# Routing products and key-value sums moved ahead in the head pairs of an attention and mixture-of-experts kernel

## The chip, the cores and the metric

The kernel runs on one core of a Trainium2 chip. A core has five engines that work through their own instruction lists in parallel: TensorE (PE; its weight loads are listed apart as PEld), VectorE (DVE), ScalarE (ACT), GpSimd (POOL) and SyncE (SP, which here only issues DMAs). The metric is the device time of one execution in microseconds (us); lower is better.

## The reference

The inputs are q, k and v of 8 batches x 8 heads x 576 positions x 64, and a 128 x 64 matrix omega. Attention is the linear kind with random features:

```python
def phi(x):
    proj = np.einsum('bhsd,md->bhsm', x, omega)
    sq = np.sum(x * x, axis=-1, keepdims=True) / 2.0
    h = proj - sq
    h = h - np.max(h, axis=-1, keepdims=True)
    return np.exp(h) / np.sqrt(m)
q_p, k_p = (phi(q_s), phi(k_s))
kv = np.einsum('bhsm,bhsd->bhmd', k_p, v)
z = np.sum(k_p, axis=2)
num = np.einsum('bhsm,bhmd->bhsd', q_p, kv)
den = np.einsum('bhsm,bhm->bhs', q_p, z)[..., None] + 1e-06
```

The 4608 rows of num / den go to a mixture of 8 experts: gate logits by a 512 x 8 matrix, the best expert of each row, and for that expert `np.maximum(xe @ w1[e], 0.0) @ w2[e]` with a hidden width of 1024, scaled by the gate's softmax weight.

## The kernel before

The program has two stages. The attention stage fills roughly the first 260 us of the profiled span, the expert stage the rest. All five engines have an order written out by hand: each engine runs its instructions in the order in which the Python code emits them, and waits at an instruction until what it needs is there.

**Units.** Attention works on 72 units, nine for each of the batches 0 to 7: one unit for the 64 last positions of all heads (h = -1), then one for each head's first 512 positions. A unit passes through these steps:

- `turns` (L148): TensorE transposes raw k and q of a later unit, and the q features of an earlier one, into the PSUM tile tt; `copies` (L183): ScalarE copies tt to SBUF.
- `unit_p` (L200): TensorE projects onto omega, into the tile pp (two buffers).
- `unit_m` (L213): VectorE takes the maxima mx (L217).
- `unit_e` (L220): ScalarE takes four exponentials for k (kp) or four for q (qp), all on line L229.
- `unit_ks` (L231): GpSimd sums the key features.

**Pairs.** `pair` (L382) handles two heads, u and w, and the work of earlier pairs beside them. Each batch has pairs k = 0 to 3, and before pair 0 a lone unit in `rest` (L368). Batch 0 has only its pairs 2 and 3 in this form, so there are 30 pairs. For pair p, `pair_kv` (L250) makes the key-value sums of pair p - 1 on TensorE in the PSUM bank "kv", and `pair_kvt` (L267) copies them out on ScalarE. `pair_fold` (L274) multiplies the copied sums of pair p - 2 by the gate matrix and the identity in the bank "nu", and copies that to SBUF as kva on ScalarE. `numbers` runs `pair_nu` (L291), two sets of numerators on TensorE, one in the bank "nu" and one in the bank "kv", and `pair_x` (L307), the divisions on VectorE that empty these banks. Each bank exists once, so every one of these steps waits until the step before it in the same bank has been read.

**Routing steps.** When a batch's rows are done (at the end of pair 1 of the next batch), its routing is put in a queue of small steps (`group`, L542): s0 copies or reduces the logits and takes the maximum, s5 subtracts and has ScalarE take an exponential (ex, L603), s1 and s2 build the one-hot choice, s3 counts ranks with TensorE products (rr) and reads them on VectorE, s4 and s6 finish rank and gate weight and write the weight to DRAM, and one step per row block builds the tile RH (two VectorE instructions). An odd batch has 12 steps and its s0 has a TensorE product (rf), an even one has 11. Batch 3 adds eight steps that choose the first expert. Steps with a TensorE product are in the set `pe`; their product uses the bank "nu". `some` takes steps from the queue:

```python
def some(self, n, products=True):
    while n and self.queue and (products or self.queue[0] not in self.pe):
        self.queue.pop(0)()
        n -= 1
```

So `some(n, False)` stops at the next step with a product. The pair takes a product step, if one is at the head of the queue, and then up to three more.

**Between the stages.** `rest` of the experts (L868) issues 6 of the first expert's 32 layer-one products per its `fill`, then all routing steps that are left but the last batch's last six, then 4 products, then those six; after that 22 products follow (L849), and the slots of all rows are worked out.

Of the kernel before, what the change touches and what calls it, by code (L numbers as in the profile page):

```python
# [57 lines left out]
class Attention:  # L58
# [309 lines left out]
    def rest(self, i, b, pre):  # L368

        rt, u = self.routing, self.units[i]  # L370
        pre.ahead(i - len(self.units))
        self.unit_p(*u)
        self.unit_m(*u)
        self.turns(i + 3, i - 2)
        self.copies(i + 3, i - 2)
        self.numbers(b * NP - 3)
        self.unit_e(*u, 0)
        self.unit_e(*u, 1)
        self.unit_ks(*u)
        rt.some(1, False)  # L380

    def pair(self, i, p, pre):  # L382

        rt, (u, w) = self.routing, self.units[i:i + 2]
        for k in range(2):
            pre.ahead(i + k - len(self.units))
        self.unit_p(*u)
        self.unit_m(*u)
        self.turns(i + 3, i - 2, pre)
        self.copies(i + 3, i - 2, pre)  # L390
        self.pair_fold(p - 2)
        self.unit_e(*u, 0)
        self.pair_kv(p - 1)
        self.unit_e(*u, 1)
        self.unit_ks(*u)
        if rt.queue and rt.queue[0] in rt.pe: rt.some(1)
        rt.some(3, False)
        self.unit_p(*w)
        self.unit_m(*w)
        self.pair_kvt(p - 1)  # L400
        self.turns(i + 4, i - 1, pre)
        self.copies(i + 4, i - 1, pre)
        self.unit_e(*w, 0)
        self.unit_e(*w, 1)
        self.unit_ks(*w)
        if p % NP < NP - 1 or p == B * NP - 1: self.numbers(p - 2)
# [718 lines left out]
```

## Time and profile before

| | |
|---|---|
| median of 3 runs | 722.06 us (721.88 to 723.95) |
| the profiled execution | 723.1 us, span from first to last instruction 721.4 us |
| mean granted TensorE clock | 0.992 |
| busy over the span | PE 678.3, PEld 610.7, DVE 342.1, ACT 352.7, POOL 255.5 us |

A row of a timeline gives the start from the beginning of the span, the duration, the engine, the line of the kernel, the operation, the tiles written and read, shapes, and how many instructions are merged. Brackets at the end say how long the engine sat idle before and what released it. On ScalarE and VectorE an instruction may start while the last one drains, so distances between starts say how fast the engine works, and durations overlap. The name of a releaser is inferred: a wait put down to `DVE de L312` ended with what stood on VectorE just then.

### The profile page before, as it was taken

Reading aid. Unit: us, or ns where it says so; the run is one execution under the profiler, and the core shown is the slowest. Engines: PE = TensorE matmul, PEld = TensorE weight load, DVE = VectorE, ACT = ScalarE, POOL = GpSimd, SP = SyncE. Lnnn points to the kernel's source line nnn. Section 1 sums busy time; section 2 is a strip of 40 time slices with the busy share of each in tenths; the row PEclk is TensorE's granted clock in tenths of the full one; section 3 lists DMA queues with packets and bytes.
Section 4 is the critical chain, followed back from the end, with each engine's and each line's share of the span. In section 5 each row is a group of like instructions: output and inputs, shape, how many; then the busy total and the mean of one; then the engine's idle time right before and its main releaser. Section 6 shows DMA issues by size and latency. Waiting matters only on the chain. (4 is left out here: it accounts for less than half of the span.)

```text
span 721.4 us, 19765 instructions
## 1 busy us (share of the span) xinstructions
PE 678.3 (94%) x7569; PEld 610.7 (85%) x7569; DVE 342.1 (47%) x790; ACT 352.7 (49%) x961; POOL 255.5 (35%) x459
## 2 busy tenths in 40 slices
PE   6899989889898989999999998999999999999995
PEld 5788879788887877888999888988989989988994
DVE  3367887788788778722221145112245245122220
ACT  6899989989989925311221144111234144111210
POOL 7456556545556632221222212211203303212221
PEclk9999999999999999999999999999999999999998
DMA  7846346627644521551112126101135125201000
GB/s 208 241 149 193 118 116 188 188 70 199 200 128 158 183 69 47 179 175 32 48 50 63 35 88 225 60 33 61 47 132 185 60 90 183 91 33 33 18 32 22
DMA packets 69506, 79.89 MB, mean 111 GB/s; under 512 B 28398, under 2 KB 52974, under 8 KB 69360
## 3 DMA queue, kind: packets, MB, share of 16 engines
q1 hardware_dynamic: 61136, 58.81, 26.5%
q0 software_dynamic: 7680, 19.04, 8.0%
q8 instruction: 87, 1.43, 0.8%
q14 instruction: 59, 0.48, 0.2%
q10 hardware_dynamic: 544, 0.13, 0.1%
HBM read 64.79 MB, written 19.55 MB: 117 GB/s over the span
## 5 line engine op out<-in xcount | busy, mean ns | idle before, releaser
L939 PE MATMUL p<-xh,w1p 128*128 128x256 f32 (+2 forms) x1104 | 156.2, 284 | 0.9 <-ACT xh L52 0.9
L939 PEld LDWEIGHTS p<-xh,w1p 128*128 128x128 f32 x1104 | 143.3, 188 | 3.0 <-ACT xh L52 1.3
L981 POOL DMA_INDIRECT out_dram<-ys,idx x36 | 36.5, 1014 | 299.9 <-DVE ys L980 207.5
L958 DVE SCALAR_TENSOR_TENSOR hl<-p,hh 128x512 fp32r<-128x512 f32 (+1 forms) x76 | 50.1, 662 | 130.1 <-ACT hh L957 128.1
L957 ACT ACTIVATE hh<-p 128x512 fp32r<-128x512 f32 (+1 forms) x76 | 43.6, 575 | 137.1 <-PE p L939 132.8
L217 DVE TENSOR_REDUCE mx<-pp 128x8 f32<-128x1024 f32 x64 | 78.0, 1219 | 32.1 <-PE pp L210 29.8
L229 ACT ACTIVATE kp<-pp,mx 128x128 f32<-128x128 f32 x256 | 86.2, 576 | 13.0 <-DVE de L312 8.6
L939 PE MATMUL p<-xl,w1p 128*128 128x256 f32 (+2 forms) x552 | 88.9, 283 | 0.0
L229 ACT ACTIVATE qp<-pp,mx 128x128 f32<-128x128 f32 x256 | 87.6, 607 | 0.0
L210 PE MATMUL pp<-om_t,tq 64*128 64x128 f32 x1024 | 74.3, 284 | 7.2 <-ACT qp L229 6.4
L245 POOL TENSOR_TENSOR k<-kp 128x256 f32<-128x256 f32 x64 | 46.5, 727 | 92.8 <-ACT kp L229 87.0
L939 PEld LDWEIGHTS p<-xl,w1p 128*128 128x128 f32 x552 | 75.7, 188 | 0.0
L210 PEld LDWEIGHTS pp<-om_t,tq 64*128 64x128 f32 x1024 | 62.1, 187 | 14.1 <-ACT qp L229 7.9
L188 ACT COPY tq<-tt 128x1024 f32<-128x1024 f32 x59 | 72.9, 1235 | 2.2 <-PE tt L146 2.2
L966 PE MATMUL p_t<-w2p,hh 128*128 128x512 f32 x152 | 61.6, 405 | 2.3 <-DVEq L986 1.9
L968 PE MATMUL p_t<-w2p,hl 128*128 128x512 f32 x152 | 60.3, 397 | 0.0
L967 PE MATMUL p_t<-w2p,hh 128*128 128x512 f32 x152 | 60.1, 395 | 0.0
L979 ACT ACTIVATE ys<-p_snu,gt 128x256 f32<-128x256 f32 x18 | 8.5, 474 | 91.9 <-PE p L939 55.5
L968 PE MATMUL p_snu<-w2p,hl 128*128 128x512 f32 x136 | 53.3, 392 | 0.0
L966 PE MATMUL p_snu<-w2p,hh 128*128 128x512 f32 x136 | 53.2, 391 | 0.0
L967 PE MATMUL p_snu<-w2p,hh 128*128 128x512 f32 x136 | 53.2, 391 | 0.0
L980 DVE TENSOR_SCALAR ys<-p_snu,gt 128x256 f32<-128x256 f32 x18 | 8.7, 484 | 85.8 <-ACT ys L979 85.8
(368 smaller groups left out, 1226.2 us busy)
## 6 DMA issues: line engine op xcount, KB each, us to landing
w1s<-in_moe_w_dram SPq DMA_DIRECT2D x5, 2048.0 KB, 8.7
w2s<-in_moe_w_dram SPq DMA_DIRECT2D x5, 2048.0 KB, 11.3
v<-in_v_dram SPq DMA_DIRECT2D x32, 256.0 KB, 4.9
token_rows<-xc SPq DMA_DIRECT2D x8, 1024.0 KB, 4.8
k<-in_k_dram SPq DMA_DIRECT2D x31, 256.0 KB, 4.9
q<-in_q_dram SPq DMA_DIRECT2D x31, 256.0 KB, 5.1
kr<-in_k_dram SPq DMA_DIRECT2D x16, 64.0 KB, 3.2
vz<-in_v_dram SPq DMA_DIRECT2D x16, 64.0 KB, 4.2
```

The lines of the kernel that those rows point to most:

```text
L188: self.nc.scalar.copy(self.pack(i, j), tt)
L210: nc.tensor.matmul(pp[:, a, n, i, :], th[r, k].rearrange("p a t -> p (a t)"), self.om[r, :], start=True, stop=True)
L217: nc.vector.tensor_reduce(out=mx[:, :, n], in_=s[("pp", h)][:, :, n], axis=AX.X, op=ALU.max, negate=True)
L229: nc.scalar.activation(x[:, j, :], pp[:, j % 2, n, j // 2, :], AF.Exp, bias=mx[:, j % 2, n, j // 2:j // 2 + 1])
L245: add = lambda o, x, y: nc.gpsimd.tensor_tensor(out=o, in0=x, in1=y, op=ALU.add)
L939: self.nc.tensor.matmul(o, w[:, i, c], x[:, i, :], start=k == 0, stop=k == len(ops) - 1)
L957: self.nc.scalar.activation(a, o, AF.Relu)
L958: self.nc.vector.scalar_tensor_tensor(out=b, in0=o, scalar=0.0, in1=a.bitcast(F32), op0=ALU.max, op1=ALU.subtract)
L966: nc.tensor.matmul(p, h, self.w2h[:, c, :], start=c == 0, stop=False)
L967: nc.tensor.matmul(p, h, self.w2l[:, c, :], start=False, stop=False)
L968: nc.tensor.matmul(p, l, self.w2h[:, c, :], start=False, stop=c == self.NF - 1)
L981: self.nc.gpsimd.indirect_dma_start(out=self.out[:, :], in_=y, in_offset=None, bounds_check=NT - 1, out_offset=bass.IndirectOffsetOnAxis(a ...
```

## The change

In `pair`, the routing steps move from behind the first unit's exponentials to a place ahead of the key-value sums, and a product step now counts among the three. `pair_kv` and its copy `pair_kvt` are emitted ahead of the fold; the copies of the sums and of the fold now stand on ScalarE between u's k exponentials and its q exponentials. In `rest` up to two steps without a product are taken, where one was.

```diff
--- before.py
+++ after.py
@@ -377,7 +377,7 @@
         self.unit_e(*u, 0)
         self.unit_e(*u, 1)
         self.unit_ks(*u)
-        rt.some(1, False)
+        rt.some(2, False)
 
     def pair(self, i, p, pre):
 
@@ -388,16 +388,17 @@
         self.unit_m(*u)
         self.turns(i + 3, i - 2, pre)
         self.copies(i + 3, i - 2, pre)
+        products = bool(rt.queue) and rt.queue[0] in rt.pe
+        rt.some(int(products))
+        rt.some(3 - products, False)
+        self.pair_kv(p - 1)
+        self.unit_e(*u, 0)
+        self.pair_kvt(p - 1)
         self.pair_fold(p - 2)
-        self.unit_e(*u, 0)
-        self.pair_kv(p - 1)
         self.unit_e(*u, 1)
         self.unit_ks(*u)
-        if rt.queue and rt.queue[0] in rt.pe: rt.some(1)
-        rt.some(3, False)
         self.unit_p(*w)
         self.unit_m(*w)
-        self.pair_kvt(p - 1)
         self.turns(i + 4, i - 1, pre)
         self.copies(i + 4, i - 1, pre)
         self.unit_e(*w, 0)
```

ScalarE, batch 4, pair 2 and the start of pair 3. tq is the copy of the transposed tile, ex the routing exponential, the other names as above. Before:

```order
L188 COPY tq_39_3271<-tt_39_3254 128x2x8x64
L288 COPY kva_3282<-fold_3273 128x146
L229 ACTIVATE kp_4_3284<-pp_4_3243,mx_4_3252 128x128 x4
L229 ACTIVATE qp_4_3300<-pp_4_3243,mx_4_3252 128x128 x4
L603 ACTIVATE ex_3318<-sh_3316 128x40
L271 COPY kvt_3340<-kv_3289 128x256
L188 COPY tq_40_3359<-tt_40_3342 128x2x8x64
L229 ACTIVATE kp_5_3361<-pp_5_3329,mx_5_3338 128x128 x4
L229 ACTIVATE qp_5_3366<-pp_5_3329,mx_5_3338 128x128 x4
L188 COPY tq_41_3433<-tt_41_3416 128x2x8x64
```

With the change, the same stretch and on into pair 3:

```order
L188 COPY tq_39_3269<-tt_39_3252 128x2x8x64
L229 ACTIVATE kp_4_3284<-pp_4_3241,mx_4_3250 128x128 x4
L271 COPY kvt_3289<-kv_3273 128x256
L288 COPY kva_3300<-fold_3291 128x146
L229 ACTIVATE qp_4_3302<-pp_4_3241,mx_4_3250 128x128 x4
L188 COPY tq_40_3340<-tt_40_3323 128x2x8x64
L229 ACTIVATE kp_5_3342<-pp_5_3312,mx_5_3321 128x128 x4
L229 ACTIVATE qp_5_3347<-pp_5_3312,mx_5_3321 128x128 x4
L188 COPY tq_41_3414<-tt_41_3397 128x2x8x64
L604 ACTIVATE ex_3424<-sh_3422 128x40
L229 ACTIVATE kp_6_3442<-pp_6_3386,mx_6_3395 128x128 x4
L271 COPY kvt_3447<-kv_3431 128x256
```

kvt and kva stand between kp and qp, and ex, which stood behind both sets of exponentials of pair 2, now stands in pair 3 ahead of kp_6.

TensorE, batch 4, pair 0, from the transposes of u to the projection of w (the products of s3 are rr, of which the first stands at the end here). Before:

```order
L146 MATMUL tt_35_2924<-ident,qp_7_2813 128x64 x8
L283 MATMUL fold_2943<-G,kvt_2787 64x72 x4
L286 MATMUL fold_2943<-ones,ks_2_2613 64x1 x4
L264 MATMUL kv_2959<-kp_6_2746,v_1690 64x128 x4
L264 MATMUL kv_2959<-kp_-1_2211,vz_158 64x128
L264 MATMUL kv_2959<-kp_-1_2211,vz_159 64x128
L264 MATMUL kv_2959<-kp_7_2808,v_1690 64x128 x4
L578 LDWEIGHTS rt_tri
L578 MATMUL rr_2980<-rt_OH,rt_tri 128x32
```

With the change, from the second-last product of s3, whose first follows the transposes `tt_35` at once:

```order
L582 LDWEIGHTS rt_ones
L582 MATMUL rr_2943<-rt_OH,rt_ones 128x16
L582 LDWEIGHTS rt_ones
L582 MATMUL rr_2943<-rt_OH,rt_ones 128x8
L264 MATMUL kv_2964<-kp_6_2750,v_1688 64x128 x4
L264 MATMUL kv_2964<-kp_-1_2181,vz_158 64x128
L264 MATMUL kv_2964<-kp_-1_2181,vz_159 64x128
L264 MATMUL kv_2964<-kp_7_2808,v_1688 64x128 x4
L283 MATMUL fold_2982<-G,kvt_2755 64x72 x4
L286 MATMUL fold_2982<-ones,ks_2_2617 64x1 x4
L210 MATMUL pp_1_3003<-om_t,tq_33_2806 128x128 x8
```

The products have moved ahead of sums and fold; the sums come behind them and the fold last.

VectorE between the stages: what stands ahead of the last batch's first step, the copy of rf into rt_L. Before, the end of the row-block steps:

```order
L628 TENSOR_SCALAR rt_RH_90<-rt_iob_93,rt_RM_89,rt_ihi_122 128x128
L628 TENSOR_SCALAR rt_RH_90<-rt_iob_93,rt_RM_89,rt_ilo_123 128x128
L628 TENSOR_SCALAR rt_RH_90<-rt_iob_93,rt_RM_89,rt_ihi_122 128x128
L628 TENSOR_SCALAR rt_RH_90<-rt_iob_93,rt_RM_89,rt_ilo_123 128x128
L558 COPY rt_L_85<-rf_7_5849 128x8
L560 TENSOR_REDUCE l_mx_5853<-rt_L_85 128x5
L601 TENSOR_TENSOR l_sh_5859<-rt_L_85,l_mx_5853 128x40
```

With the change, the stretch behind the last reduction of attention:

```order
L629 TENSOR_SCALAR rt_RH_90<-rt_iob_93,rt_RM_89,rt_ihi_122 128x128
L629 TENSOR_SCALAR rt_RH_90<-rt_iob_93,rt_RM_89,rt_ilo_123 128x128
L561 TENSOR_REDUCE mx_6_5805<-rt_L_85 128x4
L602 TENSOR_TENSOR sh_6_5807<-rt_L_85,mx_6_5805 128x32
L565 TENSOR_TENSOR w_6_5811<-rt_L_85,mx_6_5805 128x32
L566 TENSOR_TENSOR w_6_5811<-w_6_5811,rt_rev_95 128x32
L568 TENSOR_REDUCE mw_6_5814<-w_6_5811 128x4
L571 TENSOR_TENSOR rt_OH_86<-w_6_5811,mw_6_5814 128x32
L573 TENSOR_REDUCE cs_6_5817<-rt_OH_86 128x8
L574 TENSOR_TENSOR rt_CU_87<-rt_CU_87,cs_6_5817 128x8
L586 TENSOR_TENSOR m_6_5826<-rr_6_5820,rt_OH_86 128x32
L588 TENSOR_REDUCE rk_6_5828<-m_6_5826 128x4
```

Ahead of `COPY rt_L<-rf_7` there are now 29 instructions behind attention's last reduction, where there were 8: the whole group of batch 6 has moved here, with its product and its exponential.

## Rows read from the trace of the kernel before

**Rows 1.** Stretch 60 to 100 us: length, then busy PE, PEld, DVE, ACT, POOL; clock.

```profile
60.00:100.00 40.00, 36.19 (x756) 33.02 (x753) 31.70 (x80) 36.03 (x114) 21.23 (x42) 1.00 0.46 131
```

**Rows 2.** Groups by line, 60 to 250 us: busy, mean ns, idle before and releasers.

```profile
L229 ACT ACTIVATE kp<-pp,mx 128x128 f32<-128x128 f32 x197 | 66.0, 564 | 12.9 <-DVE de L312 8.6 <-DVE mx L217 4.3
```

**Rows 3.** Timeline of ScalarE, batches 1 to 7; mostly batch 4.

```profile
41.98 1.32 ACT L188 COPY tq<-tt 128x1024 f32<-128x1024 f32 x1
...
138.77 1.14 ACT L229 ACTIVATE kp<-pp,mx 128x128 f32<-128x128 f32 x4 [1.38 <-DVE de L312]
...
140.78 1.06 ACT L188 COPY tq<-tt 128x1024 f32<-128x1024 f32 x1
...
143.85 0.51 ACT L271 COPY kvt<-kv 128x256 f32<-128x256 f32 x1
...
144.10 1.17 ACT L188 COPY tq<-tt 128x1024 f32<-128x1024 f32 x1
...
147.01 1.24 ACT L188 COPY tq<-tt 128x1024 f32<-128x1024 f32 x1
...
147.91 0.53 ACT L288 COPY kva<-fold 128x146 f32<-128x146 f32 x1
...
148.08 1.40 ACT L229 ACTIVATE kp<-pp,mx 128x128 f32<-128x128 f32 x4
...
150.38 0.26 ACT L603 ACTIVATE ex<-sh 128x40 f32<-128x40 f32 x1
...
153.10 1.14 ACT L229 ACTIVATE kp<-pp,mx 128x128 f32<-128x128 f32 x4 [1.30 <-DVE de L312]
...
229.27 1.14 ACT L188 COPY tq<-tt 128x1024 f32<-128x1024 f32 x1
```

**Rows 4.** Timeline of VectorE, batch 4.

```profile
131.36 1.23 DVE L217 TENSOR_REDUCE mx<-pp 128x8 f32<-128x1024 f32 x1
...
134.44 0.19 DVE L585 TENSOR_TENSOR m<-rr,rt_OH 128x32 f32<-128x32 f32 x1 [1.86 <-PE rr L581]
...
137.47 1.21 DVE L217 TENSOR_REDUCE mx<-pp 128x8 f32<-128x1024 f32 x1
...
145.60 0.46 DVE L314 TENSOR_TENSOR x<-nu,de 128x288 f32<-128x288 f32 x1
...
149.14 0.17 DVE L558 COPY rt_L<-rf 128x8 f32<-128x8 f32 x1 [1.17 <-PE rf L557]
...
151.79 1.22 DVE L217 TENSOR_REDUCE mx<-pp 128x8 f32<-128x1024 f32 x1
```

**Rows 5.** Timeline of TensorE, batch 4.

```profile
134.14 0.18 PE L578 MATMUL rr<-rt_OH,rt_tri 128*128 128x32 bf16 x1 [0.68 <-ACT kva L288]
...
144.42 0.73 PE L301 MATMUL nu<-kva,tq 128*64 128x73 f32 x16 [0.32 <-ACT kvt L271]
...
145.07 1.16 PE L210 MATMUL pp<-om_t,tq 64*128 64x128 f32 x16
...
146.31 0.42 PE L146 MATMUL tt<-ident,qp 64*128 64x64 f32 x8
...
146.66 0.47 PE L283 MATMUL fold<-G,kvt 128*64 128x72 f32 x8
...
147.17 0.64 PE L264 MATMUL kv<-kp,v 128*64 128x128 f32 x8
...
148.49 0.61 PE L557 MATMUL rf<-lr,rt_fold 128*128 128x8 f32 x4
...
149.03 1.16 PE L210 MATMUL pp<-om_t,tq 64*128 64x128 f32 x16
```

**Rows 6.** Timeline of VectorE between the stages.

```profile
266.12 0.17 DVE L558 COPY rt_L<-rf 128x8 f32<-128x8 f32 x1 [0.76 <-PE rf L557]
...
267.36 0.20 DVE L570 TENSOR_TENSOR rt_OH<-l_w,l_mw 128x40 bf16<-128x40 f32 x1
```

**Rows 7.** Timeline of TensorE between the stages.

```profile
268.10 9.74 PE L849 MATMUL p<-x,w1s 128*128 128x256 f32 x44
```

## The prediction

> **What bounds the kernel now.** I read the busy time by stretches first. In attention PE and ACT are equally busy, 36.2 and 36.0 of 40 us, and DVE is at 31.7 [rows 1]. So no engine is full, and the question is who waits for whom. The groups by line answer it for ScalarE: nearly all of its idle time stands ahead of one group, the k exponentials, 12.9 us in 190, and what it waits for is VectorE [rows 2].
>
> The timeline of ScalarE then shows what it does when it doesn't wait. From the copy at 140.78 to the copy at 147.01, one pair, it runs at 6.23 us; from 144.10 to 147.01, one unit without extras, at 2.91 [rows 3]. Six batches lie between the copies at 41.98 and 229.27, that is 187.3 us. At ScalarE's own pace they would take 6 x (4 x 6.23 + 2.91) = 167.0; six routing exponentials last 0.26 each, 1.6, partly over their neighbours, so I add 1.1: 168.1. 19.2 us are lost there, and that is all that a better order in the loop can give.
>
> Where it goes is seen in batch 4. Stall A: kp at 138.77 waits 1.38 us (and the copies ahead of it already started late), stall B: kp at 153.10 waits 1.30 [rows 3]; both for maxima that VectorE starts at 137.47 and 151.79 only [rows 4]. VectorE is late there because of routing: it waited 1.86 us for the products rr, worked through 11 small instructions, and only then took w's maximum; at B it waited 1.17 us for rf [rows 4]. And rr was late because its bank was freed by ScalarE's copy kva: PE stood 0.68 us idle for it [rows 5]. ScalarE waits for VectorE, which waits for TensorE, which waited for ScalarE.
>
> TensorE has its own small wait of this kind: the second numerators wait 0.32 us for kvt [rows 5], since kvt and they share a bank and kvt is copied only at 143.85, after the q exponentials [rows 3].
>
> **The change, part by part.**
>
> *Products first.* They now follow the transposes. At A these end where the maximum of u is being taken, from 131.36 for 1.23 us [rows 4], so rr is done before VectorE wants it, at 132.6 in place of 134.44. That takes 1.86 us off w's maximum; the step that leaves the pair takes two RH instructions more. A needs 1.38 + about 0.4, so it goes. At B the wait of 1.17 goes, and s2 leaves the pair; B goes too. A third place like A lies in pair 3 of the same batch. What is late next is ScalarE itself.
>
> *At most three steps, two in the lone unit.* Every pair has less routing between two maxima. Price: s2 now stands in the lone unit right ahead of pair 0, which also has s3. I take 0.3 us in each of three batches, 0.9 (bounds 0 and the 0.63 that s2's three instructions last at the spacing worked out below, so 0 to 1.9).
>
> *Sums before the fold, kvt ahead of q.* On TensorE the same work stands between the transposes of u and those of w, only in another order: fold 0.51 us (146.66 to 147.17), sums 1.32 (147.17 to 148.49), rf 0.54 [rows 5]. The second numerators' wait for kvt goes, so PE gets further ahead. ScalarE now reaches kvt 0.90 + 1.0 us after the start of the copy of u (147.01 to 147.91 for the copy, half of 138.77 to 140.78 for four exponentials), and kva 0.25 later (143.85 to 144.10) [rows 3]. The transposes end 0.28 ahead of that copy (146.31 + 0.42 against 147.01); sums, then fold end 1.83 us after them, so 1.55 after the copy's start, 0.6 ahead of ScalarE. With a product it is 0.54 more and the margin about nothing. I count no wait at the 19 pairs without a product, and 0.5 us in all at the 11 with one, for the 36 products of the first expert's choice above all (bounds 0 and 11 x 1.17, the wait that VectorE had for rf, if ScalarE inherits it: 12.9).
>
> *The routing exponential.* This is the cost that the description doesn't name: ex is emitted with its step, so it now stands on ScalarE ahead of u's k exponentials, six times in the loop. If VectorE is late, all of ScalarE stands. From rt_L at 149.14 to ex at 150.38 there are 1.24 us [rows 3, 4]. u's maximum at A's pair ended at 132.59 [rows 4], 0.8 before ScalarE wanted it, so 1.24 - 0.8 = 0.45 is lost when VectorE is on time, and 1.3 when it is as tight as at 148.08, just behind a maximum. I take 0.5 each, 3.0 in all (bounds 0 and 7.8).
>
> [...]
>
> *The end of attention.* With fewer steps per pair the queue runs late, and batch 6's whole group is left for the stretch between the stages. There VectorE has 21 instructions more ahead of rt_L. Six such steps took from 266.12 to 267.36, 0.21 each [rows 6]; 21 make 4.4, less the 0.76 that VectorE waited for rf anyway, 3.7. At the pace of the 11 instructions from 134.44 to 137.47, 0.28 [rows 4], it is 5.1. Nothing hides it: the next 22 expert products start at 268.10 [rows 7] behind the last batch's products, for which VectorE must first come to its one-hot choice; TensorE stands meanwhile. Gate-weight DMAs on SP's queue move by up to a batch with their steps; no load stands right behind one that needed it earlier, so I count them at nothing, and GpSimd's order is unchanged. The expert stage behind it is untouched and shifts as a whole.
>
> Sum: 19.2 - (0.9 + 0.5 + 3.0) = 14.8 gained in the loop, 3.7 lost behind it: 11.1. Against the profiled execution of 723.1 this gives 712.0, against the median of 722.06, 711.0. I predict **711.5**.
>
> **Rivals.**
>
> *Everything goes.* If TensorE, freed from kvt, gets far enough ahead that ex and the fold never hold ScalarE, 19.2 are gained: 723.1 - 15.5 = 707.6, or 706.6 by the median. For it: stretches like 138.77 to 150.38 already run without a wait. Against: TensorE's pair takes 3.42 (145.07 to 149.03 less rf) + 1.59 + 2 x 0.65 = 6.3 us, as much as ScalarE's, so it gains only in pair 3, which has no numerators.
>
> *The wait turns round (slower).* ScalarE's queue now holds two copies and ex ahead of exponentials, where before only VectorE stood. At the six ex 1.3 each, at the 11 pairs with a product 1.17 each: 20.7, more than the 19.2 that can go. With the 3.7 behind: 723.1 + 1.5 + 3.7 = 728, 727 by the median. It decides as soon as these 17 places lose more than 1.04 us each (17.7 in all, which leaves 1.5 against 3.7). Half of that, 0.5 to 1 each, ends near no change. For it: the margin of the fold with a product is nil. Against: in such a pair ex and fold wait for the same late VectorE, so their waits overlap, and a late ScalarE lets TensorE catch up.
>
> *The tail is worse.* If TensorE's products for batch 6 and the exchange with ScalarE double the 3.7, the time is 715, still faster.
>
> **How the numbers follow.** The forecast (with the worse tail) 0.66, its own range 707.5 to 719; everything goes 0.14, time 705.5 to 707.5; the wait turns round 0.20, of which 0.10 lands slower, 0.06 within the bound and 0.04 still faster. About 0.3% (2.2 us) is what a measurement tells from no change. A further 0.02 of the forecast lies between 719 and 720, within the bound. So faster 0.82, same 0.08, slower 0.10. The range from 705.5 to 720 leaves out the 0.10 that is slower, half of what lands within the bound, and some 0.03 below.
>
> **What would show it.** Right: the copies of batches 1 to 7 that stand at 41.98 and 229.27 come 12 to 17 us closer together; rr and rf no longer appear as VectorE's releasers for more than 0.3 us; kvt no longer appears ahead of the second numerators; ScalarE shows waits of 0.3 to 0.8 ahead of ex; rt_L between the stages comes 3.5 to 5 us later after attention's last reduction, with TensorE idle ahead of the last rr. Wrong: waits of over 1 us ahead of ex or kva, with the fold as releaser, at most pairs with a product; or k exponentials that still wait over 1 us for VectorE.

## The result and the profile after

The changed kernel takes 709.91 us (median of 4 runs, 708.92 to 714.09) against 723.0 of the kernel before in the same comparison (4 runs, 721.88 to 724.0). The ratio is 0.984, 95% interval 0.9815 to 0.9866: faster by 1.3 to 1.9%. The forecast was 711.5 (705.5 to 720). The profiled execution has 709.2 us and a span of 707.5; its mean granted clock is 0.996, against 0.992 before.

The stretch that answers to [rows 1] shows TensorE a little busier and ScalarE without a gap:

```profile
60.00:100.00 40.00, 36.98 (x795) 34.88 (x793) 31.11 (x82) 40.00 (x127) 24.22 (x48) 1.00 0.60 180
```

The groups of ScalarE by line, 60 to 235 us, answer to [rows 2]. The 12.9 us listed ahead of the k exponentials are 0.3, and neither of the two copies that moved ahead of the q exponentials has taken them over:

```profile
L229 ACT ACTIVATE kp<-pp,mx 128x128 f32<-128x128 f32 x194 | 72.1, 711 | 0.3 <-DVE mx L217 0.2
...
L271 ACT COPY kvt<-kv 128x256 f32<-128x256 f32 x24 | 16.5, 686 | 0.0
L288 ACT COPY kva<-fold 128x146 f32<-128x146 f32 x24 | 14.8, 617 | 0.0
```

ScalarE's timeline (start, duration), with the first and the last copy of the same rank as in [rows 3], and pairs 1 and 2 of batch 3 from 106.53 on:

```profile
40.10 1.42 ACT L188 COPY tq<-tt 128x1024 f32<-128x1024 f32 x1
...
106.53 0.80 ACT L288 COPY kva<-fold 128x146 f32<-128x146 f32 x1
106.69 1.68 ACT L229 ACTIVATE qp<-pp,mx 128x128 f32<-128x128 f32 x4
107.70 1.57 ACT L188 COPY tq<-tt 128x1024 f32<-128x1024 f32 x1
108.60 1.72 ACT L229 ACTIVATE kp<-pp,mx 128x128 f32<-128x128 f32 x4
...
110.61 1.65 ACT L188 COPY tq<-tt 128x1024 f32<-128x1024 f32 x1
112.01 1.29 ACT L229 ACTIVATE kp<-pp,mx 128x128 f32<-128x128 f32 x4
...
114.46 1.23 ACT L188 COPY tq<-tt 128x1024 f32<-128x1024 f32 x1
...
213.64 1.37 ACT L188 COPY tq<-tt 128x1024 f32<-128x1024 f32 x1
```

The two copies stand 173.54 us apart, where they stood 187.29: the loop gives 13.75. One wait shows without a bracket: kp starts 1.40 after its copy at 110.61, where 0.90 is the pace (107.70 to 108.60).

VectorE in the places that answer to [rows 4]: the end of that pair 1, and then stall A's place, pair 0 of batch 4:

```profile
108.28 0.17 DVE L312 TENSOR_SCALAR de<-nu 128x5 f32<-128x5 f32 x1 [0.32 <-PE nu L304]
...
110.05 0.62 DVE L526 TENSOR_REDUCE rt_L<-x 128x32 f32<-128x256 f32 x1
110.59 0.20 DVE L533 TENSOR_REDUCE lr<-x 128x8 f32<-128x32 f32 x1
110.70 1.21 DVE L217 TENSOR_REDUCE mx<-pp 128x8 f32<-128x1024 f32 x1
...
125.64 1.23 DVE L217 TENSOR_REDUCE mx<-pp 128x8 f32<-128x1024 f32 x1
126.78 0.18 DVE L586 TENSOR_TENSOR m<-rr,rt_OH 128x32 f32<-128x32 f32 x1
...
129.12 1.22 DVE L217 TENSOR_REDUCE mx<-pp 128x8 f32<-128x1024 f32 x1 [0.28 <-PE pp L210]
```

The read of rr at 126.78 follows u's maximum without a wait (before 1.86), and w's maximum starts 2.34 later, when its projection is there. TensorE, to [rows 5]: rr runs under u's maximum, sums and fold behind it; the second numerators wait for kvt only once more between 40 and 240 us (0.7), but the first ones now wait for kva.

```profile
107.38 0.73 PE L301 MATMUL nu<-kva,tq 128*64 128x73 f32 x16 [0.27 <-ACT kva L288]
...
125.95 0.19 PE L579 MATMUL rr<-rt_OH,rt_tri 128*128 128x32 bf16 x1
...
126.16 0.66 PE L264 MATMUL kv<-kp,v 128*64 128x128 f32 x8
...
127.31 0.42 PE L283 MATMUL fold<-G,kvt 128*64 128x72 f32 x8
```

Between the stages, to [rows 6, 7], attention's last logits reduction and the copy of rf on VectorE, then TensorE:

```profile
247.59 0.62 DVE L526 TENSOR_REDUCE rt_L<-x 128x32 f32<-128x256 f32 x1
...
254.11 0.46 DVE L559 COPY rt_L<-rf 128x8 f32<-128x8 f32 x1
```

```profile
251.38 1.97 PE L850 MATMUL p<-x,w1s 128*128 128x256 f32 x8
255.92 0.18 PE L579 MATMUL rr<-rt_OH,rt_tri 128*128 128x40 bf16 x1 [2.57 <-DVE rt_OH L571]
...
256.40 5.86 PE L850 MATMUL p<-x,w1s 128*128 128x256 f32 x26
```

From the reduction to the 22 products it is now 8.81 us; before it was 5.26, from this row to the products at 268.10 [rows 7]:

```profile
262.84 0.62 DVE L525 TENSOR_REDUCE rt_L<-x 128x32 f32<-128x256 f32 x1
```

So the 13.9 us between the two profiled executions come out as: loop 13.75 gained; between the stages 3.55 lost; from the last copy to attention's last reduction 0.38 lost (33.57 before, 33.95 now); ahead of the first copy 1.88 gained; from the 22 products to the end 2.2 gained (453.3 and 451.1). The last two aren't the change's: the rows at the end of this document with a clock of 0.57 and 0.72 belong to them. The order itself is worth some 10 us.

### The profile page after: what moved, and what is told of

It is laid out like the page before. It is cut to its first block, busy times and chain, and to the rows that moved or that the text cites. A ratio compares the mean times of both kernels' runs of the same rounds, so it can differ in the third digit from the quotient of the medians.

```text
span 707.5 us, 19748 instructions
## 1 busy us (share of the span) xinstructions
PE 668.1 (94%) x7569; PEld 607.3 (86%) x7569; DVE 339.7 (48%) x790; ACT 352.9 (50%) x961; POOL 255.8 (36%) x459
## 5 line engine op out<-in xcount | busy, mean ns | idle before, releaser
L229 ACT ACTIVATE qp<-pp,mx 128x128 f32<-128x128 f32 x256 | 96.3, 737 | 0.0
L229 ACT ACTIVATE kp<-pp,mx 128x128 f32<-128x128 f32 x256 | 93.8, 695 | 0.3 <-DVE mx L217 0.2
L188 ACT COPY tq<-tt 128x1024 f32<-128x1024 f32 x59 | 83.1, 1408 | 0.9 <-PE tt L146 0.9
```

The lines of the kernel that those rows point to most:

```text
L188: self.nc.scalar.copy(self.pack(i, j), tt)
L229: nc.scalar.activation(x[:, j, :], pp[:, j % 2, n, j // 2, :], AF.Exp, bias=mx[:, j % 2, n, j // 2:j // 2 + 1])
```

## The experiments

For each kernel the table has the median with its ratio to the kernel before and the 95% interval, then, from its profiled execution, the distance of the two copies ("loop"), and that from attention's last reduction to the 22 products ("tail").

| kernel | us | ratio | loop | tail |
|---|---|---|---|---|
| before | 721.6 to 723.6 | 1 | 187.29 | 5.26 |
| changed | 709.91 | 0.984 (0.9815 to 0.9866) | 173.54 | 8.81 |
| routing only | 715.93 | 0.9922 (0.9903 to 0.9941) | 177.84 | 8.83 |
| sums only | 732.26 | 1.0145 (1.0123 to 1.0166) | 200.48 | 5.26 |
| cap only | 723.53 | 1.0025 (1.0000 to 1.0049) | 180.29 | 8.82 |
| old counts | 709.82 | 0.9836 (0.9812 to 0.986) | 175.93 | 5.25 |
| reductions later | 709.92 | 0.9842 (0.982 to 0.9864) | 173.02 | 8.82 |
| ex behind | 713.45 | 0.9878 (0.9849 to 0.9907) | 173.14 | 10.09 |
| plan | 713.34 | 0.9876 (0.9857 to 0.9895) | 176.95 | 6.90 |
| plan, reductions early | 709.43 | 0.9828 (0.9805 to 0.985) | 176.01 | 5.25 |
| reductions later, ex behind | 711.35 | 0.985 (0.9825 to 0.9874) | 172.77 | 8.82 |
| plan, ex behind | 707.33 | 0.9795 (0.9772 to 0.9818) | 173.91 | 5.26 |

The runs of one kernel lie 1 to 7 us apart, so differences of 1 to 2 us are read from the two right columns.

### Taking the change apart

*Routing only* (against the kernel before):

```diff
-        rt.some(1, False)
+        rt.some(2, False)
...
+        products = bool(rt.queue) and rt.queue[0] in rt.pe
+        rt.some(int(products))
+        rt.some(3 - products, False)
         self.pair_fold(p - 2)
         self.unit_e(*u, 0)
         self.pair_kv(p - 1)
         self.unit_e(*u, 1)
         self.unit_ks(*u)
-        if rt.queue and rt.queue[0] in rt.pe: rt.some(1)
-        rt.some(3, False)
```

> Only the routing part of the change: the steps follow the transposes, at most three with a product counted, two in the lone unit; the fold, the key-value sums and their copies stay in their old order. Theory A (the parts need each other: the gain comes from VectorE no longer waiting for routing products; their bank must be free when they come, and the sums and kvt in front free TensorE): 716 us, range 712 to 720. The tail between the stages gets 3.6 us longer as in the changed kernel, the k exponentials keep about 0.3 to 0.5 us of wait per pair with a product, and the second numerators still wait for kvt. Theory B (the gain is the routing alone: the order of sums and fold is worth nothing): 709 to 711, as the changed kernel. Theory C (the gain is from kvt and the sums freeing TensorE, routing does nothing but lengthen the tail): 724 to 727.

Theory A, in the time, the tail and the wait for kvt. The waits that it saw ahead of the k exponentials aren't listed; instead the distance from u's copy to w's in pair 3 grows by up to 0.9 us. In the waits of TensorE, 40 to 240 us (engine and line, waited for; total, times, longest), a new one is on top:

```profile
PE fold L283 <- DVE m L586: 5.7, 6, 1.3
PE nu L301 <- ACT kvt L271: 2.8, 4, 0.8
```

rr stands in the bank "nu" ahead of the fold now, so the fold waits until VectorE has read rr, and sums and projection of w queue behind it. The second row is the old wait for kvt.

*Sums only* (against the changed kernel):

```diff
-        rt.some(2, False)
+        rt.some(1, False)
...
-        products = bool(rt.queue) and rt.queue[0] in rt.pe
-        rt.some(int(products))
-        rt.some(3 - products, False)
...
         self.unit_ks(*u)
+        if rt.queue and rt.queue[0] in rt.pe: rt.some(1)
+        rt.some(3, False)
         self.unit_p(*w)
```

> Only the other part: key-value sums and kvt ahead of the fold and of the q exponentials; the routing steps at their old place and in their old number. The fold's copy kva now comes about 1.25 us later than before, and the routing products wait for it in the same bank. Theory A: the loop gets slower, 725 to 732 us, with VectorE waiting over 2.5 us ahead of the first read of the routing products and the k exponentials of w waiting for that; the tail between the stages stays as short as before. Theory B (routing alone is the gain): 721 to 724, no change. Theory C (the sums are the gain): 706 to 710, since the tail isn't lengthened.

Theory A again, just above its range: the same instructions, 10 us slower than before. Waits of TensorE and VectorE, 40 to 240 us:

```profile
PE rr L578 <- ACT kva L288: 9.2, 6, 2.1
```

```profile
DVE m L585 <- PE rr L581: 15.3, 6, 3.2
```

Before, TensorE's rr waited 0.68 at the place shown [rows 5]; with kva behind kp and kvt it waits up to 2.1, and VectorE up to 3.2. So the two halves are not two gains. Moved alone, the routing products hold the fold; moved alone, the fold holds the routing products. Together the product is in front, the sums fill the time in which VectorE reads it, and the fold finds the bank free (127.31 above, without a wait).

A part of this loss is the clock. The first of these waits of rr, and the granted clock (third-last column) just behind it:

```profile
71.64 0.18 PE L578 MATMUL rr<-rt_OH,rt_tri 128*128 128x32 bf16 x1 [2.05 <-ACT kva L288]
```

```profile
73.20:76.60 3.40, 3.40 (x52) 3.13 (x50) 3.16 (x13) 2.17 (x7) 0.00 (x0) 0.50 0.18 28
```

Five such stretches lie in this loop, none in that of the kernel before. u's interval in pair 2, from its copy to w's, takes 6.04 us in the batch in which one of them falls there, and 5.38 and 5.39 in two without. At this 0.66 each, they would be some 3 of the 13.2 us that the loop grew, an estimate; the rest is the waits themselves.

*Cap only* (the kernel before with the change's numbers of steps):

```diff
-        rt.some(1, False)
+        rt.some(2, False)
...
-        if rt.queue and rt.queue[0] in rt.pe: rt.some(1)
-        rt.some(3, False)
+        products = bool(rt.queue) and rt.queue[0] in rt.pe
+        rt.some(int(products))
+        rt.some(3 - products, False)
```

> The old order of everything; only the number of routing steps is that of the changed kernel, three in a pair with the product among them, two in the lone unit. Theory A (where the products stand is what counts): VectorE still waits 1 to 2 us for each routing product, some steps fewer stand behind it, and the tail is 3.6 us longer: 717 to 722 us. Theory B' (the gain comes from fewer steps between two maxima): 710 to 714, and VectorE's wait for the products is still there but no longer reaches the k exponentials.

No gain, a little above what theory A gave. But the table shows that the loop did gain 7.0 us. It was lost behind it: 3.56 in the tail, 3.9 from the last copy to the last reduction (37.46 against 33.57, a part of it with the clock at 0.91 in 240 to 250). VectorE's wait for rr, 40 to 240 us, in the kernel before and here, and then ScalarE's for VectorE [rows 2]:

```profile
DVE m L585 <- PE rr L581: 8.0, 6, 1.9
```

```profile
DVE m L586 <- PE rr L582: 8.7, 5, 1.9
```

```profile
ACT kp L229 <- DVE de L312: 4.4, 5, 1.2
```

VectorE's wait for rr is as long as before; it reaches the exponentials less, because fewer steps stand behind it.

*Old counts* (the changed kernel with the old numbers):

```diff
-        rt.some(2, False)
+        rt.some(1, False)
...
-        rt.some(3 - products, False)
+        rt.some(3, False)
```

> The changed kernel with the old numbers of steps: a product and up to three more in a pair, one in the lone unit. Theory A (the place counts, not the number): the loop loses some tenths at the pairs with four steps, about 0.4 to 0.6 us at each of 8 to 10 places, and the tail gets back the 3.55 us that the change lost there: 708 to 713 us. Theory B' (the number counts): the loop's gain falls away, 718 to 723. In both the products between the stages should follow attention's last reduction by about 5.3 us in place of 8.8.

Theory A. The place alone brings 11.4 of the loop's 13.75, and the number 2.4 more on top of it (alone, in *cap only*, it brought 7.0: the two gains overlap); but the number also costs the whole 3.55 of the tail. TensorE between the stages, to be held against the row at 256.40 above (the reduction starts at 250.01):

```profile
254.91 0.18 PE L579 MATMUL rr<-rt_OH,rt_tri 128*128 128x40 bf16 x1
...
255.26 6.94 PE L850 MATMUL p<-x,w1s 128*128 128x256 f32 x31
```

The wait of 2.57 is gone. In time the two kernels can't be told apart.

### What is left in the loop

From one copy to the next the pace without a wait is 6.30 for pair 0, 3.34 for u and 2.91 for w of the other pairs, 2.91 for the lone unit: 27.96 a batch, 167.8 in six. The change leaves 5.8 above this. In its trace most of it, 4.1, stands at one place: u's interval in pair 2 takes 3.78 to 4.38 instead of 3.34. There the two reductions of the finished batch stand ahead of u's maximum (110.05 and 110.59 above), and they come late in part because the first numerators waited 0.27 for kva (107.38 above). I hadn't seen this place.

*Reductions later* (in `pair`; `sums` does what `pair_x` did at the end of a batch):

```diff
         self.copies(i + 3, i - 2, pre)
+        self.sums()
         products = bool(rt.queue) and rt.queue[0] in rt.pe
```

> The changed kernel, with the two logits reductions of a finished batch (0.66 us on VectorE) behind the maximum of u of pair 2 instead of ahead of it; every pair takes the same routing steps. Theory A (what is still lost in the loop, 5.4 us, is mostly the k exponentials of pair 2 waiting for that maximum): the span between the two copies falls from 173.5 to 170 to 171.5 us, the time to 706.5 to 708.5. Theory E (ScalarE would wait there anyway, since TensorE or the maximum of w is late next): 709 to 711, no change.

Theory E: 0.5 us. The interval fell to 3.33 to 3.35 in five batches, and the loss appeared elsewhere: pair 3's u takes up to 3.99 where it took 3.34 to 3.47, pair 0 up to 0.3 more and in the last batch 0.8. In pair 3, ScalarE and VectorE:

```profile
87.44 1.88 ACT L188 COPY tq<-tt 128x1024 f32<-128x1024 f32 x1
88.86 0.60 ACT L613 ACTIVATE ex<-sh 128x40 f32<-128x40 f32 x1
89.00 1.49 ACT L229 ACTIVATE kp<-pp,mx 128x128 f32<-128x128 f32 x4
```

```profile
87.07 1.21 DVE L217 TENSOR_REDUCE mx<-pp 128x8 f32<-128x1024 f32 x1
...
88.62 0.20 DVE L611 TENSOR_TENSOR sh<-rt_L,mx 128x40 f32<-128x40 f32 x1
```

Here ex is what I had priced: 1.42 after the copy instead of 0.90, held by sh.

*ex behind* (s5 only notes the exponential; `flush` emits it; its place in `pair`):

```diff
         self.unit_e(*u, 0)
+        rt.flush()
         self.pair_kvt(p - 1)
```

> The changed kernel, with the routing exponential ex emitted behind u's k exponentials instead of ahead of them, as the only edit. The prediction's price (0.5 us at each of six places): 706.5 to 707.5. Theory F (VectorE has the difference ready before ScalarE gets there, except at two places with 0.9 and 0.5): the loop gains 0.5 to 1.4 us, 708.5 to 709.9, hardly to be told from no change.

The loop gained 0.4, as theory F has it. The total came out slower than either theory: its tail is 10.09, and the clock is 0.71 in 245 to 250 (row at the end), so this says little about ex.

*Both edits together*:

> The changed kernel with both small edits at once: the logits reductions behind u's maximum in pair 2, and ex behind u's k exponentials. The trace of the first edit alone shows the loss of pair 2 gone and 0.1 to 0.7 us new in pair 3, where ex waits for a VectorE that now comes later. Theory G (the loss only moved, from the k exponentials of pair 2 to ex of pair 3; with both ways closed it goes): the span between the two copies 169.5 to 171, the time 706 to 708. Theory E (TensorE is late next whatever the order): 172.5 to 174 and 709 to 711.

Theory G falls: 172.77. With ex and the reductions out of the way pair 3's u still takes 3.33 to 3.80, pair 0 up to 7.42.

Theory E named TensorE as the reason. It can be tried directly (on the changed kernel, and on the version with both edits):

```diff
-                (0, v0[:, 2, :], k0[:, 2, :], 0, 0, 0), (0, v0[:, 3, :], k0[:, 3, :], 1, 0, 1),
+                (0, v0[:, 3, :], k0[:, 3, :], 1, 0, 1),
...
-                (1, v1[:, 0, :], k1[:, 0, :], 0, 1, 0), (1, v1[:, 1, :], k1[:, 1, :], 1, 0, 0),
+                (1, v1[:, 0, :], k1[:, 0, :], 0, 1, 0),
```

> The changed kernel with two of the ten key-value products of each pair left out (a quarter of one head's positions of each kind is missing from the sums, so rows go to other experts and only the span between the two copies is to be compared). TensorE has about 0.13 us less per product, 0.26 per pair, 6.2 over the 24 pairs between the copies. Theory E (TensorE's own pace is what is left in the loop): 173.5 falls to 168 to 171. Theory H (ScalarE is back to back and at its own pace, or VectorE's reductions alone make the loss): 172.5 to 173.5.

> The same two products left out of the version with later reductions and ex behind the k exponentials (the same part of the computation is missing). Theory E: 172.8 falls to ScalarE's own pace, 167.2 plus 0.1 to 0.2 at each ex, so 167.5 to 169.5, lower than the other kernel of this pair by 1 to 2 us. Theory H: 172 to 173.

The loops took 173.50 and 172.79 us: to 0.04 the same as with all products. (The totals, 717.84 and 717.93, belong to another distribution of rows.) TensorE's wait from 45 to 205 us, first in the changed kernel, then with fewer products:

```profile
PE nu L301 <- ACT kva L288: 3.7, 13, 0.5
```

```profile
PE nu L301 <- ACT kva L288: 7.7, 15, 0.9
```

What TensorE saved it spent for the most part waiting for kva. So TensorE's work isn't the bound of the loop, however full it looks. Theory H has the number, but its reasons aren't shown either: ScalarE at its own pace would take 167.8, and with the reductions out of the way the loss stayed. What the rows suggest instead is a ring: kva (106.53), numerators (107.38), divisions (108.28), u's maximum (110.05 without the reductions), kp (1.31 later, as 110.70 to 112.01), that is 111.36; ScalarE's own pace would bring kp at 111.51. A ring with 0.15 to spare pays for nearly everything that is put into it, wherever it stands. The products left out don't stand in it. That fits seven versions with 172.8 to 173.9 (the three others with the products in front, *old counts* and the first two plans below, take 175.9 to 177.0), but it is argued; no run shortened the ring.

### Another plan of steps

*Plan*: instead of a number per pair, fixed places (`sums` stands behind `self.unit_m(*w)` of pair 2; `beside` takes the steps of the first choice):

```diff
-        products = bool(rt.queue) and rt.queue[0] in rt.pe
-        rt.some(int(products))
-        rt.some(3 - products, False)
+        k, b = p % NP, p // NP
+        rt.some({0: 3, 1: 5, 2: 0, 3: 4}[k])
+        if k == 2 and b in (5, 6):
+            rt.beside({5: 4, 6: 2}[b])
```

> A fixed plan of steps instead of a number per pair: s0 s5 s1 s2 in pair 3, s3 s4 s6 in pair 0, all row blocks in pair 1, nothing in pair 2 and the lone unit, but the eight steps of the first choice in pair 2 of batch 5, the lone unit and pair 2 of batch 6; the logits reductions stand in pair 2 behind w's maximum. The queue is empty after each period, so that only four row-block steps are left between the stages. Theory A (loop and tail losses are separate and both come from where steps stand): 1.5 to 3 us in the loop and 3.5 in the tail, 703 to 706 us. If four steps in pair 3 or five row blocks in pair 1 make w's maximum late, 0.5 to 1 us at each of 10 places: 708 to 713, with the tail still 3.5 shorter.

> The same plan with the logits reductions behind u's maximum in pair 2 instead of behind w's. Theory A: the same within 1 us, 703 to 706; slower than the other only if pair 2, with the first choice's steps beside the reductions in batches 5 and 6, makes w's maximum late (up to 1 us at two places). In the other order the divisions of pair 2 come 0.66 us later, which would show as a wait of the products of pair 3 for the bank.

Neither reached theory A's 703 to 706. The first landed at the upper end of its worse case: with s0 and s5 in pair 3, that u takes 4.30 to 4.86. Its tail of 6.90 holds a stretch of lower clock (0.57 in 253 to 257), so it doesn't say what the plan's tail is worth. The second has 3.46 to 4.30 there and the short tail, but 3.83 for w of the two pairs 1 that take five row blocks. The repaired one, against the second:

```diff
         k, b = p % NP, p // NP
+        rt.some((3, 4, 1, 4)[k])
         if k == 2:
+            rt.beside({5: 3, 6: 1, 7: 2}.get(b, 0))
             self.sums()
-        rt.some({0: 3, 1: 5, 2: 0, 3: 4}[k])
-        if k == 2 and b in (5, 6):
-            rt.beside({5: 4, 6: 2}[b])
...
         self.unit_e(*u, 0)
+        rt.flush()
```

> The fixed plan with the reductions behind u's maximum, with three repairs: ex behind u's k exponentials, at most four row blocks in pair 1 (the fifth in pair 2), and the steps of the first choice as f0 f1 f2 in pair 2 of batch 5, f3 f4 in the lone unit, f5 in pair 2 of batch 6, f6 f7 in pair 2 of batch 7. Theory G: the span between the copies 169 to 171.5 (before this 176.0), the products between the stages 5.2 us after the last reduction as in the kernel before, 702 to 705 us. Theory E: 173 to 175 and 706 to 709, from the shorter tail alone.

Theory E for the loop (173.91), and the tail as in the kernel before. TensorE and VectorE between the stages:

```profile
253.59 0.18 PE L602 MATMUL rr<-rt_OH,rt_tri 128*128 128x40 bf16 x1
...
253.94 8.23 PE L876 MATMUL p<-x,w1s 128*128 128x256 f32 x37
```

```profile
248.68 0.62 DVE L540 TENSOR_REDUCE rt_L<-x 128x32 f32<-128x256 f32 x1
```

At 707.33 us (706.32 to 711.08) this is the fastest version: the tail's 3.55 back, 0.7 lost ahead of the last reduction, 0.4 in the loop. Its interval and the changed kernel's still touch, so the 2.6 us between their medians are likely, not certain.

## Why the prediction was right

**The bound, and the loop.** ScalarE waited for VectorE, VectorE for rr, rr for kva: *sums only* makes the last link longer (up to 2.1 in place of 0.68) and the loop grows with it (200.48 against 187.29). 14.8 us were forecast for the loop, 13.75 came. The pace was read from one pair and taken for all; pair 0 takes 6.30 without a wait (40.10 to 46.40), not 6.23, so that the floor was 0.4 too low.

**Products first.** Stalls A and B are gone, as said: pair 0 of batch 4 falls from 8.48 to 6.30, w's interval in pair 2 from 4.35 to 2.91. The place alone gives 11.4 of 13.75 (*old counts*). The number alone gives 7.0 in the loop and nothing in the time (*cap only*), and on top of the place 2.4, less than the tail that it costs.

**Two or three steps.** 0.9 was taken for s2 in the lone unit. Pair 0 takes 6.56 and 6.62 in two batches instead of 6.30, 0.6 in all.

**Sums, kvt, fold.** Forecast 0.5; ScalarE shows no wait ahead of kva or kvt. I hadn't followed kva one step further, to the first numerators: 3.7 us of TensorE's time in 160, and with the reductions behind them most of what is left. In the sum this cancelled against the next term, which is luck.

**ex.** This was mis-sized: 3.0 forecast, 0.5 each. Five ex fall into the loop, the sixth behind it. Three, in pair 3, lengthen u's interval by 0.13, their own time on ScalarE, which stays when they are moved; one in batch 6, together with f5, goes with 0.7, and one with a part of the 1.04 in batch 1's pair 2. That is 1.1 to 2.1 in all; moving ex gave 0.4. Nor had I counted what ex cost at its old place: in the kernel before it started 1.29 us after the q exponentials (149.09 and 150.38), where 1.00 is the pace, and u's interval in pair 2 was 3.75 to 3.76 in the five batches with an ex there, so that the move also took away some 0.4 at each place that it left. The reason given, that ScalarE stands behind an ex whose sh is late, does show where VectorE is tight (88.86 above): kp stands behind ex there and starts 0.14 after it, though its own maximum had ended at 88.28 (87.07 and 1.21).

**The tail.** Forecast 3.7, measured 3.55, with TensorE idle 2.57 us ahead of the last rr. *Old counts* and the last plan get it back, so the reason was the number of steps left over.

**The signs.** Most came. Two did not: no wait ahead of ex is listed, where 0.3 to 0.8 were forecast, and rt_L comes 6.52 us after attention's last reduction, where it came 3.28 after it, so 3.24 later and not 3.5 to 5.

**The rivals.** The turned wait didn't come: fold and kvt hold nobody in the changed order. It is what *routing only* shows for TensorE (5.7 us), because there the fold stands directly behind the product.

**The time.** 711.5 against 709.91. The order's share by the two traces, 9.8 us, is less than the 11.1 forecast; the rest of the 13.1 between the medians lies in what the executions have beside it, the lower clock of the last section (0.57 and 0.72) among it. That the forecast came so near is in part luck.

## What to carry to other kernels

Two steps that share a buffer are one change: moving either alone only turned the wait round here (the fold waited 5.7 us for VectorE, rr 9.2 for kva), so ask of each who must have read the buffer before it. When the steps per turn are capped, count what is left at the end, for here nothing covered it (3.55 us). And before a fuller engine is called the bound, take work away from it and see whether the time moves (here the loop moved by 0.04 us at most).

## What I had not expected of the hardware

In the profiled executions the granted TensorE clock fell for a few microseconds, at other places in one than in another: to 0.57 and 0.72 in the kernel before, and to 0.71 in *ex behind*. Windows of the kernel before, of the changed kernel, of *ex behind*, and of the kernel before once more (the third-last column is the clock):

```profile
24.00:28.00 4.00, 3.72 (x52) 3.61 (x52) 0.20 (x1) 2.63 (x8) 0.30 (x1) 0.57 1.08 303
```

```profile
24.00:28.00 4.00, 4.00 (x90) 3.85 (x92) 0.54 (x1) 3.31 (x11) 1.10 (x2) 1.00 1.13 298
```

```profile
245.00:250.00 5.00, 3.12 (x27) 2.55 (x23) 4.00 (x18) 0.23 (x1) 1.59 (x4) 0.71 0.13 51
```

```profile
446.00:452.00 6.00, 5.55 (x17) 4.43 (x18) 0.30 (x1) 0.00 (x0) 0.00 (x0) 0.72 0.39 147
```

In 24 to 28 us the first has 0.57 and the second 1.00, and the first copy of the kernel before comes 1.88 later than that of the changed kernel. In the 4 us ahead of it TensorE had been busy 1.88 us, in the changed kernel 1.58, and there the clock stayed at 1.00. *Cap only*, which has the old order ahead of that copy, has it at 40.06, so the 1.88 isn't the change's. The plan with early reductions had it at 42.35 with a clock of 1.00 in 20 to 30 us; the clock isn't the only reason for a late start.

The last row lies in the expert stage, which the change leaves alone. From the 22 products to the end the kernel before takes 453.3 us and *cap only*, whose clock falls there too, 453.3 (both have 0.98 in 400 to 500 us); the changed kernel and the last plan, without such a stretch (1.00 there), take 451.1 and 450.7. So most of the 2.2 us there goes with the clock and not with the order. In *sums only* it doesn't look like chance alone: each of its five stretches begins within 2 us after a wait of TensorE for kva of 1.80 to 2.05 us ended, though another of 1.96 us (206.89) has none, and all four of its runs have a mean of 0.985 to 0.987, those of the changed kernel 0.991 to 0.996.

The listed durations on ScalarE grew while it ran back to back, at the same pace: the same copy lists 1.57 us at 107.70, with the next instruction 0.90 later, and only 1.23 at 114.46, soon behind a wait, with the next instruction again 0.90 later. So the mean duration of the k exponentials, which rises from 564 ns [rows 2] to 711, is no slowdown here.
